# Six tiles for the first evictions, V's weights asked for behind x, two more blocks of Q ahead of the maxima

## The chip, the core and the metric

One core of a Trainium2 chip. Its engines run side by side: TensorE (PE, with its weight loads as PEld), VectorE (DVE), ScalarE (ACT), GpSimd (POOL) and SyncE (SP), which issues nearly all DMAs here. The metric is the device time of one execution in microseconds (us). The kernel before takes 1442.8 us (median of three runs, 1441.62 to 1445.62).

## The reference

Two branches of one input `x` (2048 x 512) are mixed by a gate per token:

```python
x = A_x
g = _sigmoid((x * gate_w).sum(-1, keepdims=True))
a = _A_ref(x, A_wqkv, A_wo)      # attention, 32 heads of 16, full softmax, then @ wo
b = _B_ref(x, B_w_r, ...)        # r = x @ w_r; the two tokens with the largest r
                                 # get a SwiGLU FFN times sigmoid(r); the rest pass x
return g * a + (1 - g) * b
```

Everything is float32. The kernel keeps float32's precision by splitting operands into a high and a low part and adding three products.

## The kernel before

A **unit** is one pair of heads and one half of the 1024-query range: 32 units of 16 **steps** (one step for each block of 128 keys). For every unit the kernel first needs the maxima of the scores (`m_piece`: TensorE products reduced by VectorE), then, some 21 steps behind (`LEAD`), come the scores again (`s_piece`: TensorE, then the exponential on ACT into a tile `P`) and the product with V (`av_mm`). The order of these is written out by hand in `ORDER`, a string that the main loop repeats every three steps: `s` a score piece, `m` a maximum, `A` the product with V, `f` one slot of other work (`slots`: the later projections, the FFN, the output projection). `at_step` hangs small pieces of work on the end of a step; steps of the lead are negative, from -21 to -1. `late` holds ACT work to be issued at the start of the next round of `ORDER`.

The **lead** is what the change touches:

- `load_w(0)` and `load_x` ask for the first weights of K and Q, for x in 16 DMAs, then for constants (`cst`) and V's weights (`wvs`). All these go through SP's queue in order. A DMA of this kernel may wait in SP for the one eight places before it.
- `split_w`, `split_x` make high and low parts: ACT the high, VectorE or POOL the low.
- `proj0` and `proj` multiply out one 512-column block of K or Q for the first four pairs (12 matmuls each into a PSUM tile `st`, of which there are three). The result is split into an eviction tile `ev` (ACT L70, VectorE L71). `first_rows` then copies the first pair's rows by four DMAs into `Kx` or `Qx` (L198, L199), and `store_ev` writes the whole block to a scratch tensor in DRAM (L172). Blocks with an odd number are evicted into `Qx[1]` or `Qx[2]`, which are not in use yet; even ones into the ring tag `ev` with two buffers.
- K's four blocks and Q's first are done up front. `lead_parts` yields the rest in parts of three matmuls: Q's block 1 (four parts), V's first two tiles (a V tile is four parts `v_part`, and ACT evicts it, L270), Q's blocks 2 and 3, the other 14 V tiles.
- The loop over the steps of the lead calls `m_lead` (four products for maxima, L583, and three reductions on VectorE, L588) and three or four of those parts.
- For the gate and the router, `load_rows` loads x by rows in four DMAs (ring tag `xs`, two buffers that x's first two blocks had), `products` multiplies on POOL (L300), `sums` adds up on ACT (L304). `r_row` transposes the router's column on TensorE (L316), and `route_rows`, `route_best`, `route_index` and `gather` find the two tokens.

Ring tags that matter: `xs` (two buffers), `P` (three: x's blocks 2 and 3, V's weights, their low part, later the score tiles), `ev` (two), `st` (three PSUM tiles), `o` (six).

Of the kernel before, what the change touches and what calls it, by code (L numbers as in the profile page):

```python
# [11 lines left out]
OP = mybir.AluOpType  # L12
# [21 lines left out]
def gated_mix(ctx: ExitStack, tc: tile.TileContext, xT, x, wqkv, wo, w_rg, w_gate, w_up, w_down,  # L34
# [9 lines left out]
    def ap(t, off, dims):  # L44
        return bass.AP(tensor=t.tensor, offset=t.offset + off, ap=dims)
# [62 lines left out]
    def load_w(g):  # L108
        ws = ring.tile([128, 2, 4, 128], F32, tag="w", name="ws", bufs=3)
        W[g] = ws  # L110
        for i in (1, 0):
            if g == 0 and i == 0:
                load_x(0)
            nc.sync.dma_start(ws[:, i], ap(wqkv, i * D + g * 128, [[3 * D, 128], [128 * 3 * D, 4], [1, 128]]))

    def split_w(g, parts=(1, 0)):
        if 1 in parts:
# [24 lines left out]
    def proj(g, which, nb, piece):  # L142
        i = "qk".index(which)
        wh, wl = W[g]
        ps = fl_tile() if g else st_tile()
        n = 0
        for terms in (((wh, xh), (wl, xh)), ((wh, xl),)):
            for c in range(4):
                for a, b in terms:
                    nc.tensor.matmul(ps, a[:, i, c, :], b[nb][:, c, :], start=n == 0, stop=n == 11)  # L150
                    n += 1
                    if n % piece == 0 and n < 12:
                        yield
        if g:
            if (g, which, nb) == (2, "q", 3):
                late.append((split_w, (3, (1,))))
                at_step(now[0] + 2, split_w, 3, (0,))
            late.append((evict, (g, which, nb, ps)))
            yield
            return  # L160
        if nb % 2:
            ev = Qx[1 if nb == 3 else 2].rearrange("p (a n) -> p a n", a=2)
        else:
            ev = ring.tile([128, 2, 512], F32R, tag="ev", name="ev", bufs=2)
        scale = 0.25 if which == "q" else 1.0
        split(ev[:, 0], ev[:, 1], ps, scale=scale)
        first_rows(which, nb, ev)
        store_ev(0, which, nb, ev)
        yield

    def store_ev(g, which, nb, ev):
        nc.sync.dma_start(  # L172
            ap(qk_scr[which], g * 128 * S + nb * 512, [[S, 128], [D * S, 2], [1, 512]]).bitcast(F32), ev.bitcast(F32))
# [27 lines left out]
    def proj0(which, nb):  # L201
        for _ in proj(0, which, nb, 12):
            pass
# [6 lines left out]
    load_w(0)  # L210
    for nb in range(1, 4):
        load_x(nb)
    nc.sync.dma_start(cst, consts)
    wvs = ring.tile([128, 4, 512], F32, tag="P", name="wvs", bufs=3)
    nc.sync.dma_start(wvs, ap(wqkv, 2 * D, [[3 * D, 128], [128 * 3 * D, 4], [1, D]]))
    def ones(k):
        for j in range(2):
            nc.gpsimd.memset(k[64 * j + 32:64 * j + 64, :].bitcast(F32), 1.0)
# [9 lines left out]
    split_x(2)  # L228
    proj0("q", 0)
    split_x(3)  # L230
    for nb in (1, 2, 3):
        proj0("k", nb)
    wv = [wvs, Kx[1].rearrange("p (c n) -> p c n", c=4),
          ring.tile([128, 4, 512], F32R, tag="P", name="wvl", bufs=3)]
    for c in range(4):
        split(wv[1][:, c], wv[2][:, c], wvs[:, c], lo_engine=nc.gpsimd if c % 2 else None)

    def load_k(pair):

# [32 lines left out]
    def lead_parts():  # L272

        v = [(t, c) for t in range(KT) for c in range(4)]
        yield from proj(0, "q", 1, 3)
        for n in range(8):
            v_part(*v.pop(0))
            yield
        for nb in (2, 3):
            yield from proj(0, "q", nb, 3)  # L280
        while v:
            v_part(*v.pop(0))
            yield
# [4 lines left out]
    def load_rows(nb):  # L288
        if nb == 0:
            rg["w"] = o_tile("wr", [128, D]), o_tile("wg", [128, D])  # L290
            for i in range(2):
                nc.sync.dma_start(rg["w"][i], ap(w_rg, i * D, [[0, 128], [1, D]]))
        t = ring.tile([128, 4, D], F32, tag="xs", name="xn", bufs=2)
        nc.sync.dma_start(t, ap(x, nb * 512 * D, [[D, 128], [128 * D, 4], [1, D]]))
        rg[nb] = t

# [17 lines left out]
    def r_row():  # L314
        ps = fl_tile((16, 128))
        nc.tensor.transpose(ps, gz[:, :, 0], ident)  # L316
        rg["row"] = ring.tile([16, 128], F32, tag="rt", name="rt", bufs=1)
        nc.scalar.activation(rg["row"], ps, AF.Copy)

    def route_rows():  # L320

# [6 lines left out]
        nc.sync.dma_start(ap(i_scr, 0, [[8, 16], [1, 8]]), idx8)  # L328

    def route_best():  # L330
        nc.vector.max(best8, cand)
        nc.vector.max_index(pos8, best8, cand)
        nc.sync.dma_start(pos2, pos8[:, 0:2])
        nc.sync.dma_start(rsel, best8[:, 0:2])
# [5 lines left out]
    def gather():  # L340
        nc.gpsimd.indirect_dma_start(out=xsel, out_offset=None, in_=x,
                                     in_offset=bass.IndirectOffsetOnAxis(ap=idx2[:, :1], axis=0))
        nc.gpsimd.memset(xselT, 0.0)
        nc.scalar.activation(rsel, rsel, AF.Exp, scale=-1.0)
        nc.vector.tensor_scalar(rsel, rsel, 1.0, None, op0=OP.add)
        nc.vector.reciprocal(rsel, rsel)

    def x_rows():
        ps = fl_tile((128, 4, 2))
# [247 lines left out]
    def m_unit(u):  # L597
        m = ring.tile([128, 2, 8], F32, tag="m", name="m", bufs=2)
        nc.vector.tensor_reduce(m, Mr[:, EL * (u % 3):EL * (u % 3) + EL].rearrange("p (t c j) -> p j t c", c=4, j=2),  # L599
                                axis=AX.X, op=OP.min)  # L600
        hl = ring.tile([128, 2, 2, 8], F32R, tag="hl", name="hl", bufs=2)
        pool_split(hl[:, :, 0], hl[:, :, 1], m)
        turn.append([3 if u < UNITS - 1 else 0, u, hl])

    turn = []
# [155 lines left out]
        for f, a in fill.pop(s, []):  # L761
            f(*a)

    for nb in range(4):
        at_step(-20 + 4 * nb, load_rows, nb)
    for t in range(16):
        at_step(-17 + t, sums, t)
    for t in range(16):
        at_step(-19 + t, products, t)
    at_step(-1, r_row)  # L770
    at_step(1, gates, 0)
    at_step(2, route_rows)
    at_step(4, gates, 1)
    at_step(10, route_best)
    at_step(16, route_index)
    at_step(22, gather)
    at_step(-8, load_w, 1)
    at_step(-5, split_w, 1)
    at_step(2, load_w, 2)
# [9 lines left out]
    order = [(w, nb) for nb in range(4) for w in "kq"]  # L789

    def slots():
        for w, nb in order:
            yield from proj(1, w, nb, 3)
        late.append((split_w, (2,)))
        at_step(now[0] + 4, load_w, 3)
        x_rows()
        yield
        for w, nb in order:
            yield from proj(2, w, nb, 3)
        for n, (w, nb) in enumerate(order):  # L800
            yield from proj(3, w, nb, 3)
            if w == "q":
                for i in range(4):
                    at_step(now[0] + i + 1, load_ff, ("gate", "up")[i // 2], (w_gate, w_up)[i // 2],
                            ("xh", "xl")[i // 2], nb, i % 2)
        yield from ff_in("gate")
        for j in range(4):
            at_step(now[0] + 2 * j, load_down, j)
        ff_t(0, "gate")
        yield  # L810
        yield from ff_in("up")
        ff_t(1, "up")
        late.append((ff_act, ()))
        at_step(now[0] + 3, ff_h)
        at_step(now[0] + 3, load_wo)
        for c in range(4):
            at_step(now[0] + 6 + c, split_wo, c)
        yield
        yield
        yield from ff_down()  # L820
        ff_sum()
        last_tiles()
        s = now[0]
        for nb in range(4):
            at_step(s + 5 + 2 * nb, load_acc, nb)
        for t in range(16):
            at_step(s + 11 + t, acc_scale, t)
        at_step(s + 1, load_at, 0, (0, 1))
        at_step(s + 4, split_at, 0, (0, 1))
        yield from wait(s + 8)  # L830
        yield from wo_groups((0, 1), (2,))
        assert now[0] > 3 * 8 * KT + 16
        yield from wo_groups((2,))
        yield from wait(STEPS - 15)
        for t in range(8, 16):
            wo_last(t, 96)
            yield
# [51 lines left out]
        for _ in range(n):  # L889
            next(parts, None)  # L890

    parts_next(4)
    for s in range(-LEAD, 0):
        now[0] = s
        if s == -11:
            load_q(1)
        m_lead(s + LEAD)
        parts_next(3 + (s < -LEAD + 4))
        end_step(s)
    count["m"] = 4 * LEAD  # L900

    while count["m"] < UNITS * EL:
        run_late()
        for o in ORDER:
            if o == "s":
                s, i = divmod(count["s"], 4)
                if i == 0:
                    start_step(s)
                s_piece(s, i % 2, i // 2)
                count["s"] += 1  # L910
                if i == 3:
                    end_step(s)
            elif o == "m":
                m_next()
            elif o == "A":
                if count["A"] < 0:
                    parts_next(3)
                p_v(count["A"])
                count["A"] += 1
            else:  # L920
                next(fills, None)
# [43 lines left out]
```

## Time and profile before

| | us |
|---|---|
| median of three runs | 1442.8 |
| the profiled execution, as timed | 1443.71 |
| its span, first to last instruction | 1441.9 |
| TensorE busy in the span | 1426.5 |
| VectorE, ACT, POOL busy | 1300.1, 1168.7, 302.5 |
| granted TensorE clock, mean | 0.998 |

The profile shows one execution. Its views used here: the page (busy time of each engine), windows (busy time by stretch, granted clock, DMA rate), the chain of waits that ended last, and timelines of an engine, where a bracket gives the idle time before an instruction and what ended it. Line numbers are those of the kernel before.

### The profile page before, as it was taken

The numbers are of one execution on the slowest core, as the hardware profiler recorded it, in microseconds if no ns is written. First come the engines' busy times: TensorE is split into PE (matmuls) and PEld (weight loads), VectorE is DVE, ScalarE is ACT, GpSimd is POOL, SyncE is SP. The second block draws the span as 40 slices with busy tenths as digits, with TensorE's granted clock in tenths as the row PEclk, the third lists the DMA queues.
The fourth block names the chain that finished last, engine by engine and source line by source line (L and its number), as shares of the span: only waits on it lengthen the run. The fifth ranks groups of instructions, "written<-read, shape, count | busy, mean of one in ns | idle before, by whom it ended". The sixth has DMA issues, their size and how long they took to land.

```text
span 1441.9 us, 24169 instructions
## 1 busy us (share of the span) xinstructions
PE 1426.5 (99%) x9141; PEld 631.9 (44%) x9141; DVE 1300.1 (90%) x1541; ACT 1168.7 (81%) x2262; POOL 302.5 (21%) x321
## 2 busy tenths in 40 slices
PE   8999999999999999999999999999999999999998
PEld 5654444444444444444444443434444444444434
DVE  5779999999999999999999999999999999999933
ACT  4468888888888888888888888888888888888874
POOL 3652000112000001200001100033832222233220
PEclk9999999999999999999999999999999999999999
DMA  8702021212214121312222342314213121111003
GB/s 265 195 21 64 20 52 31 53 45 41 53 53 107 61 53 31 67 31 64 57 81 52 98 104 70 86 42 130 73 31 68 35 53 27 32 31 38 25 17 117
DMA packets 53475, 92.71 MB, mean 64 GB/s; under 512 B 12972, under 2 KB 24300, under 8 KB 51856
## 3 DMA queue, kind: packets, MB, share of 16 engines
q1 hardware_dynamic: 53264, 91.17, 24.4%
q8 instruction: 72, 1.18, 0.4%
q14 instruction: 43, 0.35, 0.1%
q0 software_dynamic: 96, 0.01, 0.0%
HBM read 63.64 MB, written 28.56 MB: 64 GB/s over the span
## 4 chain that ended last, share of the span: by engine, by line
PE 95%; DMA 2%; DVE 1%; SPq 1%; ACT 0%; issue 0%; POOL 0%; DVEq 0%; POOLq 0%; ACTq 0%
PE av L633 35%; PE st L624 23%; PE mxa L556 12%; PE mxb L556 10%; PE fl L150 6%; PE fl L481 4%; PE st L268 3%; DMA xs<-xT 1%; PE mxa L583 1%; DVE Mr L560 1%; DMA wvs<-wqkv 1%; PE fl L372 0%; DVE acc L529 0%; PE st L150 0%; ACT P L625 0%; SPq L615 0%
## 5 line engine op out<-in xcount | busy, mean ns | idle before, releaser
L625 ACT ACTIVATE P<-st 128x512 f32<-128x512 f32 x2028 | 1064.5, 599 | 206.9 <-PE st L624 112.9
L560 DVE TENSOR_REDUCE Mr<-mxa 128x2 f32<-128x1024 f32 x655 | 794.9, 1214 | 3.8 <-PE mxa L556 3.5
L633 PE MATMUL av<-P,V 128*32 128x512 f32 x4096 | 545.5, 605 | 0.0
L624 PE MATMUL st<-Qx,Kx 50*128 50x512 f32 x2028 | 536.2, 443 | 2.0 <-ACT P L625 2.0
L560 DVE TENSOR_REDUCE Mr<-mxb 128x1 f32<-128x512 f32 x654 | 451.9, 691 | 63.5 <-PE st L624 18.1
L624 PEld LDWEIGHTS st<-Qx,Kx 50*128 50x128 f32 x2028 | 274.6, 184 | 234.6 <-ACT P L625 215.0
L556 PE MATMUL mxb<-Kx,Qx 48*128 48x512 f32 x654 | 325.3, 497 | 0.0
L556 PE MATMUL mxa<-Kx,Qx 48*128 48x512 f32 x1310 | 296.7, 420 | 1.2 <-DVE Mr L560 1.2
L556 PEld LDWEIGHTS mxb<-Kx,Qx 48*128 48x128 f32 x654 | 119.5, 183 | 273.7 <-DVE Mr L560 254.4
L556 PEld LDWEIGHTS mxa<-Kx,Qx 48*128 48x128 f32 x1310 | 125.1, 183 | 52.2 <-DVE Mr L560 10.3
L633 PEld LDWEIGHTS av<-P,V 128*32 128x32 f32 x4096 | 80.9, 108 | 140.3 <-issue 134.7
L186 POOL TENSOR_SCALAR ev<-pe 128x512 fp32r<-128x512 f32 x24 | 35.7, 1490 | 321.3 <-ACT pe L184 321.3
L74 POOL TENSOR_SCALAR hl<-m 128x16 fp32r<-128x16 f32 x32 | 8.1, 253 | 441.1 <-DVE m L599 441.0
L448 POOL TENSOR_TENSOR acc<-acc,w 128x512 f32<-128x512 f32 x32 | 41.0, 1281 | 185.8 <-ACT w L447 171.6
L150 PE MATMUL fl<-xh,wh 128*128 128x512 f32 x96 | 42.9, 447 | 0.0
L150 PE MATMUL fl<-xh,wl 128*128 128x512 f32 x96 | 40.4, 421 | 0.0
L529 DVE SCALAR_TENSOR_TENSOR acc<-fl,gg,acc 128x512 f32<-128x512 f32 x15 | 11.3, 750 | 26.6 <-PE fl L481 26.6
L481 PE MATMUL fl<-woh,ahl 128*128 128x512 f32 x96 | 35.1, 447 | 0.0
L588 DVE TENSOR_REDUCE Mr<-mxa 128x2 f32<-128x1024 f32 x21 | 25.7, 1223 | 9.8 <-PE mxa L583 9.8
L150 PE MATMUL fl<-xl,wh 128*128 128x512 f32 x96 | 32.6, 421 | 0.0
L187 POOL TENSOR_TENSOR ev<-pe,ev 128x512 fp32r<-128x512 f32 x24 | 30.8, 1283 | 2.0
L270 ACT ACTIVATE V<-st 128x512 f32<-128x512 f32 x16 | 9.6, 598 | 25.4 <-PE st L268 25.4
(177 smaller groups left out, 781.4 us busy)
## 6 DMA issues: line engine op xcount, KB each, us to landing
Qx<-q_scr SPq DMA_DIRECT2D x62, 128.0 KB
Kx<-k_scr SPq DMA_DIRECT2D x30, 256.0 KB
k_scr<-ev SPq DMA_DIRECT2D x14, 512.0 KB
q_scr<-ev SPq DMA_DIRECT2D x14, 512.0 KB
xs<-xT SPq DMA_DIRECT2D x16, 256.0 KB
xn<-x SPq DMA_DIRECT2D x4, 1024.0 KB
Qx<-hr SPq DMA_DIRECT2D x256, 2.0 KB
acc<-x_scr SPq DMA_DIRECT2D x4, 1024.0 KB
```

Source lines behind the costliest of these rows:

```text
L150: nc.tensor.matmul(ps, a[:, i, c, :], b[nb][:, c, :], start=n == 0, stop=n == 11)
L186: nc.gpsimd.tensor_scalar(ev[:, 0], t, 1.0, None, op0=OP.mult)
L187: nc.gpsimd.tensor_sub(ev[:, 1], t, ev[:, 0].bitcast(F32))
L268: nc.tensor.matmul(ps, a[nb][:, c, sl], b[:, c, :], start=c == 0 and n == 0, stop=c == 3 and n == 2)
L448: nc.gpsimd.tensor_add(a, a, w)
L481: nc.tensor.matmul(ps, a[:, sl], b[:a.shape[0], c, :], start=first and n == 0, stop=last and n == 2)
L556: nc.tensor.matmul(dst, Qx[u % 3][64 * j:64 * j + 48, t * 128:t * 128 + 128], Kx[(u // 2) % 2][64 * j:64 * j + 48, c * 512:c * 512 + 512], ...
L560: nc.vector.tensor_reduce(Mr[:, g0:g0 + (2 if r == 1 else 1)], MX[r - 1], axis=AX.X, op=OP.max, negate=True)
L588: nc.vector.tensor_reduce(*r, axis=AX.X, op=OP.max, negate=True)
L624: nc.tensor.matmul(ps, k, q, start=True, stop=True)
L625: nc.scalar.activation(P[s][:, 2 * j + c, :], ps, AF.Exp)
L633: nc.tensor.matmul(AV[0][32 * ct:32 * ct + 32, :], V[:, kt, h * VW:h * VW + 32], P[s][:, ct, :], start=kt == 0, stop=kt == KT - 1)
```

## The change

Eviction: the blocks of K and Q of the first group get up to six tiles: two from `ev`, and two tiles of tag `xs` that hold two evictions each (`ev0`). The stores to scratch of K's blocks are collected in `scr` and issued behind the row copies of the next Q block. Order: after Q's first block only K's block 1 comes ahead of the split of V's weights; then K's blocks 2 and 3 and Q's 1 and 2 run ahead of the first maxima; only Q's block 3 stays in the lead. V's weights are asked for directly behind x; the constants move to just ahead of the lead's loop. All four low parts of V's weights are made on POOL. x's first two row blocks are loaded into tag `P`, ahead of Q's block 2 being stored; `products` and `sums` are hung one step earlier. The router's transpose is the first of the fill slots, and its other work moves accordingly. Unit 0's split of the maxima is on VectorE. On the host, the weights of K, Q and V are laid out in the order in which they are loaded (2 KB, and 8 KB for V, in one piece for each partition, where there were pieces of 512 bytes and of 2 KB).

```diff
-            nc.sync.dma_start(ws[:, i], ap(wqkv, i * D + g * 128, [[3 * D, 128], [128 * 3 * D, 4], [1, 128]]))
+            nc.sync.dma_start(ws[:, i], ap(wqkv, (2 * g + i) * 128 * D, [[D, 128], [128, 4], [1, 128]]))
...
-        if nb % 2:
-            ev = Qx[1 if nb == 3 else 2].rearrange("p (a n) -> p a n", a=2)
-        else:
-            ev = ring.tile([128, 2, 512], F32R, tag="ev", name="ev", bufs=2)
+        ev = ev0(which, nb)
         scale = 0.25 if which == "q" else 1.0
         split(ev[:, 0], ev[:, 1], ps, scale=scale)
         first_rows(which, nb, ev)
-        store_ev(0, which, nb, ev)
+        scr.append((0, which, nb, ev))
+        if which == "q":
+            if nb == 2:
+                load_rows(0)
+                load_rows(1)
+            for e in scr:
+                store_ev(*e)
+            scr.clear()
         yield
+    scr, evs = [], []
+    def ev0(which, nb):
+        if (which, nb) in (("k", 1), ("k", 3)):
+            t = ring.tile([128, 2, 2, 512], F32R, tag="xs", name="evx", bufs=2)
+            evs.extend([t[:, 0], t[:, 1]])
+        if evs:
+            return evs.pop(0)
+        return ring.tile([128, 2, 512], F32R, tag="ev", name="ev", bufs=2)
...
-    nc.sync.dma_start(cst, consts)
     wvs = ring.tile([128, 4, 512], F32, tag="P", name="wvs", bufs=3)
-    nc.sync.dma_start(wvs, ap(wqkv, 2 * D, [[3 * D, 128], [128 * 3 * D, 4], [1, D]]))
+    nc.sync.dma_start(wvs, ap(wqkv, 8 * 128 * D, [[4 * D, 128], [D, 4], [1, D]]))
...
-    for nb in (1, 2, 3):
-        proj0("k", nb)
+    proj0("k", 1)
...
-        split(wv[1][:, c], wv[2][:, c], wvs[:, c], lo_engine=nc.gpsimd if c % 2 else None)
+        split(wv[1][:, c], wv[2][:, c], wvs[:, c], lo_engine=nc.gpsimd)
...
-        yield from proj(0, "q", 1, 3)
-        for n in range(8):
-            v_part(*v.pop(0))
-            yield
-        for nb in (2, 3):
-            yield from proj(0, "q", nb, 3)
+        yield from proj(0, "q", 3, 3)
...
-        t = ring.tile([128, 4, D], F32, tag="xs", name="xn", bufs=2)
+        t = ring.tile([128, 4, D], F32, tag="P" if nb < 2 else "xs", name="xn", bufs=3 if nb < 2 else 2)
...
-        nc.scalar.activation(rg["row"], ps, AF.Copy)
+        late.append((nc.scalar.activation, (rg["row"], ps, AF.Copy)))
...
-    for nb in range(4):
-        at_step(-20 + 4 * nb, load_rows, nb)
+    at_step(-13, load_rows, 2)
+    at_step(-9, load_rows, 3)
     for t in range(16):
-        at_step(-17 + t, sums, t)
+        at_step(-18 + t, sums, t)
     for t in range(16):
-        at_step(-19 + t, products, t)
-    at_step(-1, r_row)
+        at_step(-20 + t, products, t)
...
     def slots():
+        r_row()
+        at_step(now[0] + 2, route_rows)
+        yield
...
-    parts_next(4)
+    for w, nb in (("k", 2), ("k", 3), ("q", 1), ("q", 2)):
+        proj0(w, nb)
+    nc.sync.dma_start(cst, consts)
...
-        parts_next(3 + (s < -LEAD + 4))
+        parts_next(3 + (s == -LEAD))
...
-                    parts_next(3)
+                    parts_next(2)
```

Left out: `route_best` loses its `max`, which is hung three steps earlier; the sigmoid of the two tokens' scores becomes `route_gate`, its addition on POOL and its reciprocal on VectorE five steps later; `pool_split` of unit 0 becomes a copy and a subtraction on VectorE; the host's permutation of `A_wqkv`.

More of the change, by code (lines that the diff above doesn't have):

```diff
@@ L330, in route_best @@
     def route_best():
-        nc.vector.max(best8, cand)
         nc.vector.max_index(pos8, best8, cand)
@@ L343, in gather, with route_gate @@
         nc.gpsimd.memset(xselT, 0.0)
-        nc.scalar.activation(rsel, rsel, AF.Exp, scale=-1.0)
-        nc.vector.tensor_scalar(rsel, rsel, 1.0, None, op0=OP.add)
-        nc.vector.reciprocal(rsel, rsel)
+    def route_gate(i):
+        if i == 0:
+            nc.scalar.activation(rsel, rsel, AF.Exp, scale=-1.0)
+            nc.gpsimd.tensor_scalar(rsel, rsel, 1.0, None, op0=OP.add)
+        else:
+            nc.vector.reciprocal(rsel, rsel)
     def x_rows():
@@ L601, in m_unit @@
         hl = ring.tile([128, 2, 2, 8], F32R, tag="hl", name="hl", bufs=2)
-        pool_split(hl[:, :, 0], hl[:, :, 1], m)
+        if u == 0:
+            nc.vector.tensor_copy(hl[:, :, 0], m)
+            nc.vector.tensor_sub(hl[:, :, 1], m, hl[:, :, 0].bitcast(F32))
+        else:
+            pool_split(hl[:, :, 0], hl[:, :, 1], m)
         turn.append([3 if u < UNITS - 1 else 0, u, hl])
@@ L762, in end_step @@
             f(*a)
-    for nb in range(4):
-        at_step(-20 + 4 * nb, load_rows, nb)
+    at_step(-13, load_rows, 2)
+    at_step(-9, load_rows, 3)
     for t in range(16):
-        at_step(-17 + t, sums, t)
+        at_step(-18 + t, sums, t)
     for t in range(16):
-        at_step(-19 + t, products, t)
-    at_step(-1, r_row)
+        at_step(-20 + t, products, t)
     at_step(1, gates, 0)
-    at_step(2, route_rows)
     at_step(4, gates, 1)
-    at_step(10, route_best)
-    at_step(16, route_index)
-    at_step(22, gather)
+    at_step(9, nc.vector.max, best8, cand)
+    at_step(12, route_best)
+    at_step(22, route_gate, 0)
+    at_step(27, route_gate, 1)
+    at_step(18, route_index)
+    at_step(24, gather)
     at_step(-8, load_w, 1)
@@ L949 @@
     consts[:, 134] = 128 * p
+    w = np.asarray(inputs["A_wqkv"]).reshape(4, 128, 3, 4, 128)
+    wqkv = np.concatenate([w[:, :, :2].transpose(3, 2, 1, 0, 4).ravel(), w[:, :, 2].transpose(1, 0, 2, 3).ravel()])
     arrays = {
-        "xT": np.ascontiguousarray(x.T), "x": x, "wqkv": np.ascontiguousarray(inputs["A_wqkv"]),
+        "xT": np.ascontiguousarray(x.T), "x": x, "wqkv": wqkv,
         "wo": np.ascontiguousarray(inputs["A_wo"]),
```

## The prediction

> **What bounds the kernel now.** I read the page first, then the windows by stage, then the chain of waits in order of time, and last TensorE's own timeline where the chain leaves it.
>
> ```profile
> span 1441.9 us, 24169 instructions
> PE 1426.5 (99%) x9141; PEld 631.9 (44%) x9141; DVE 1300.1 (90%) x1541; ACT 1168.7 (81%) x2262; POOL 302.5 (21%) x321
> core 0: us, PE busy (x) PEld busy (x) DVE busy (x) ACT busy (x) POOL busy (x), PEclk, DMA share, GB/s
> 6.25:24.17 17.92, 17.55 (x74) 13.13 (x72) 11.85 (x18) 12.23 (x22) 5.82 (x4) 1.00 0.98 338
> 24.17:33.30 9.13, 5.46 (x22) 3.25 (x21) 5.60 (x8) 2.88 (x6) 3.09 (x2) 0.99 0.80 190
> 33.30:95.00 61.70, 61.70 (x269) 40.97 (x268) 49.78 (x65) 29.97 (x81) 43.11 (x36) 0.97 0.51 137
> 140.00:1400.00 1260.00, 1257.71 (x8309) 536.80 (x8305) 1177.69 (x1376) 1064.90 (x2043) 232.84 (x255) 1.00 0.22 55
> 1400.00:1442.00 42.00, 35.78 (x205) 16.56 (x197) 16.15 (x27) 21.80 (x44) 2.57 (x2) 0.97 0.27 100
> ```
>
> TensorE is the bound, with 2.3 us idle in the 1260 us of the main loop, so nothing in the lead matters unless it takes idle or slow time from TensorE. The one stage with idle time that the change touches is 24.17 to 33.30 (3.7 us of 9.1). The tail's 6.2 us idle is not touched.
>
> ```profile
> 13.07 7.56 DMA wvs<-wqkv
> 20.65 0.59 SPq L198
> ...
> 27.85 1.78 DMA Kx<-ev
> 29.67 0.60 ACT Qx L70
> 30.30 0.69 DVE Qx L71
> 30.99 1.14 DVE Mr L588
> 32.18 0.51 PE mxa L583 x2
> 33.32 4.45 PE st L268 x12
> ...
> 41.37 0.43 PE mxa L583 x2
> ...
> 44.98 0.43 PE mxa L583 x2
> ...
> 47.92 0.43 PE mxa L583 x2
> 48.62 2.27 PE st L268 x9
> 50.89 0.43 PE mxa L583 x2
> ```
>
> SP waits for V's weights until 20.65 and then issues eleven copies, one each 0.655 us (20.65 to 27.85). The eviction of Q's second block (L70) waits for the copies out of the buffer it reuses, VectorE's half of it (L71) stands ahead of the first maxima (L588), and TensorE waits for those. TensorE's timeline gives the two gaps, the window after them the clock:
>
> ```profile
> 26.36 0.46 PE L583 MATMUL fl<-Kx,Qx 48*128 48x512 f32 x1 [1.68 <-DMA Kx<-Qx]
> 32.18 0.51 PE L583 MATMUL mxa<-Kx,Qx 48*128 48x512 f32 x2 [1.98 <-DVE Mr L588]
> 33.28:36.70 3.42, 3.42 (x10) 2.70 (x10) 2.37 (x4) 0.00 (x0) 0.00 (x0) 0.53 0.86 215
> 94.73 0.27 PE L316 MATMUL fl<-cst,gz 128*16 128x128 f32 x1
> 96.11 0.50 PE L624 MATMUL st<-Qx,Kx 50*128 50x512 f32 x1 [0.68 <-ACT P L625]
> ```
>
> **What the first stage would take unobstructed.** A step of the lead with three V parts takes 2.97 (47.92 to 50.89), of which 2.27 are nine matmuls, or 0.757 a part; the later steps take 2.93, so its maxima cost 0.66. A step with a whole Q block takes 3.61 (41.37 to 44.98): 2.95 beside the maxima. From 24.17 to 94.73 the old lead does 21 steps of maxima (13.9), two Q blocks (5.9) and 59 V parts (44.7): 64.4 us of work in 70.6. So 6.2 us are lost: 3.7 in the two gaps, some 1.4 to the halved clock (twelve matmuls in 4.45 where 3.03 is the pace), the rest in slow maxima beside the gaps.
>
> **Part 1: evictions, order, queue.** Six buffers take away the wait of L70, and the old VectorE chain with it. SP's order becomes: rows of K0 and Q0, their two stores, sixteen row copies (K1, K2, K3, Q1), four stores, the two rows of the router, then x's rows 0 and 1. SP still stands at Q0's last row copy until V's weights have landed. I put that landing at 20.0 instead of 20.65:
>
> ```profile
> 2.00:2.50 0.50, 0.50 (x3) 0.23 (x2) 0.00 (x0) 0.00 (x1) 0.50 (x1) 1.00 0.68 194
> 10.00:12.00 2.00, 2.00 (x9) 1.51 (x9) 2.00 (x4) 1.89 (x4) 0.00 (x0) 1.00 1.04 400
> 15.92 0.39 PE L150 MATMUL st<-xh,wh 128*128 128x512 f32 x1
> ...
> 18.64 0.39 PE L150 MATMUL st<-xh,wh 128*128 128x512 f32 x1
> ```
>
> The first window holds only the weights' 512-byte pieces: 285 GB/s when all engines are busy (194/0.68), against 385 for x's 2 KB pieces (400/1.04). For 256 KB that is 0.92 against 0.68 us, so two loads give 0.5; the constants (67.5 KB, now asked for later, first used at the router's transpose after the lead) give 0.17 more. The bounds are 0 and 1.4 (the same at 194 and 400 without the shares). TensorE's first products wait for x, so Q's second block ends about 0.4 earlier, at 23.75. [...]
>
> Then Q's third block (2.72, the spacing of two blocks, 15.92 to 18.64) runs where the first gap was, until 26.47. The first two K1 copies are issued 0.65 earlier than now but behind one more store of 512 KB, 1.33 us at the 393 GB/s below: 0.7 later than now, at 27.05, where TensorE wants them at 26.9. I take 0.15 us. VectorE's halves of K2, K3, Q1 and Q2 are done by 27.8 at the latest (26.47, and 0.60 and 0.69 as L70 and L71 took), and the maxima behind them follow with 0.5 us of slack a step (row at 77.76 below), so nothing waits there. The rest of the lead is 21 steps (13.9), the last Q block (2.95) and 60 V parts (45.4): it would end at 88.7 where the old one ends at 94.73, with one V part more behind it.
>
> **Part 2: the new wait.** The sums of the router and gate (L304, ACT) are asked for one step earlier, and stand in ACT's order ahead of V's evictions: the third V tile (V2) behind sums 0, V3 behind sums 1 and 2. ACT stops there until POOL has multiplied, and POOL until x's first rows are in. Behind ACT wait V2 and V3, and with three PSUM buffers TensorE's V5 needs V2 gone and V6 needs V3 gone.
>
> ```profile
> 35.98 0.58 SPq L172 DMA_DIRECT2D q_scr<-Qx  x1
> 36.61 0.47 SPq L292 DMA_DIRECT2D wr<-w_rg  x1
> 34.00:34.50 0.50, 0.50 (x3) 0.40 (x2) 0.50 (x2) 0.00 (x0) 0.00 (x0) 0.50 1.03 393
> 38.00:40.50 2.50, 2.50 (x13) 1.80 (x10) 2.26 (x3) 0.40 (x1) 0.00 (x0) 1.00 1.17 108
> 24.67:26.36 1.69, 0.01 (x3) 0.03 (x1) 1.54 (x2) 1.22 (x3) 1.38 (x2) 1.00 0.70 125
> 24.98 3.09 POOL L68 TENSOR_TENSOR wvl<-wvs,Kx 128x512 fp32r<-128x512 f32 x2 [5.43 <-ACT Kx L67]
> 46.61 1.29 POOL L300 TENSOR_TENSOR p<-xn,wr 128x512 f32<-128x512 f32 x1 [18.54 <-DMA xn<-x]
> 47.87 1.28 POOL L300 TENSOR_TENSOR p<-xn,wg 128x512 f32<-128x512 f32 x1
> 49.81 0.58 ACT L270 ACTIVATE V<-st 128x512 f32<-128x512 f32 x1
> 77.76 1.23 DVE L588 TENSOR_REDUCE Mr<-mxa 128x2 f32<-128x1024 f32 x1 [0.51 <-PE mxa L583]
> ```
>
> Now, Q1's store is issued at 35.98 and POOL starts 10.6 us later: store, the two router rows (at 108 GB/s, the slow part) and x's rows. In the new order the first of four stores is the nineteenth issue after 20.0, at 32.45, and three stores (4.0 us at 393 GB/s) stand ahead of Q1's. POOL starts at 32.45 + 4.0 + 10.6 = 47.1. V2 is out 3.8 us after POOL's start (46.61 to 50.39), at 50.9; V3 has four more products of 1.25 ahead of it: 8.8 after, at 55.9. TensorE wants V5 at 26.47 + 3.6 + 6 x 2.93 + 0.66 + 1.51 = 49.8 and V6 at 26.47 + 3.6 + 8 x 2.93 + 0.66 = 54.2. So it stops for 1.1 us and then 0.6, 1.7 in all. Later tiles keep ahead: four V parts take 3.9 us, the 1.33 pairs of products between them 3.35. From V6 the lead has 2.27 + 11 x 2.93 = 34.5 left: it ends at POOL's start + 43.3 = 90.4. The 0.15 for K1 is inside that.
>
> **Part 3: small edits.** V's four low parts all on POOL: 1.55 each (two in 3.09 at 24.98), 6.2 us from 20.6, done by 27 where V begins at 30; without that cover the wait would be up to 3 us. Unit 0's split on VectorE: two tiny operations (bound 0 to 0.5) inside the 0.51 slack of that stage. The router's transpose (0.27) leaves the lead's end for a fill slot; every later fill group moves three steps back, which the list's wait before its last groups takes up (bound: one slot, 0.9 us). The router's vector operations moved or split: 0 to 0.35 gained. In the first main steps one V tile half open no longer holds a score buffer: of the 0.68 at 96.11 I count 0.4 back, against the missing V part as a bound (0.76 lost).
>
> **Sum.** Old end of lead 94.73, new 90.4: 4.3. One V part more done by then: 0.75. First main steps: 0.4. Less the transpose in its slot, 0.2. Together 5.25 us. The profiled execution took 1443.7 us, of which 1.8 lie around its span; it comes to 1438.45. Its time is 0.9 above the median of the runs (1442.8), against which I predict 1437.6.
>
> **Rivals.** (B) No stop for the sums: the rows arrive by 45.4, when the router's rows, no longer mixed with stores, run at 385 instead of 108 GB/s (512 KB: 1.4 for 4.9 us). For: the 108 was seen in one place only. Against: both read one 2 KB row for 128 partitions, and that does not change. Then the lead ends at 88.7: 7.0 us, 1435.8. (C) The K1 copies become the wait: the extra store at 125 GB/s (24.67 to 26.36, mixed with row copies) takes 4.2 us, they land at 29.9 instead of 27.05, TensorE stops 3.0 us, and a window at half clock follows as at 33.28 (1.6): the lead ends at 93.3, gain 2.4, 1440.4. [...] Here the clock halved after gaps of 1.7 and 2.0, so I keep it. (D) Slower: the four stores back to back run at 125 GB/s. Each takes 4.2 instead of 1.33, POOL starts 11.5 us later, at 58.6, ACT holds V2 and V3, and TensorE stops about 13 us: 6.2 us lost, 1449.0. It is slower than now from a POOL start of 52.3 on. For: 125 is in the trace. Against: there SP's issues, not the stores, set the rate; at 34.0 a store ran at 393.
>
> **How the numbers follow.** Forecast 0.48 (POOL's start good to 1.2 us: 1436.4 to 1438.8), B 0.25, C 0.20, D 0.07. The range runs from B less the 0.35 of the router, 1435.2, to C with 0.6 for the missing V part, 1441.0; outside are D and the edges of B and C. A measurement of this kernel tells 0.3%, 4.3 us, from no change: faster means below 1438.5. That has 0.7 of the forecast, most of B and a little of C: 0.61. Slower by as much is most of D, 0.05. Within: 0.34.
>
> **What would show it.** No wait of L70 for a copy before 30 us, no gap above 0.5 us on TensorE until 48, no clock under 1.0 after 6; POOL's first product at 47.1 (45 to 48.3); two waits of TensorE for V's evictions, 1.1 near 50 and 0.6 near 55; lead's end near 90.4. A first product before 45.4 makes B, a gap for K1 near 27 makes C; a first product after 52, or a stop at the main loop's unit starts, makes me wrong altogether.

## The result, and the profile after

| | before | after |
|---|---|---|
| median of six runs, us | 1444.2 | 1454.43 |
| lowest to highest | 1441.62 to 1447.26 | 1453.86 to 1455.21 |
| span of the profiled execution | 1441.9 | 1452.1 |
| first exponential of the main loop (ACT) | 95.46 | 103.48 |

The ratio is 1.0074 (interval 1.0063 to 1.0084): the changed kernel is slower by some 10 us, where 5 us of gain were forecast. The line numbers from here on are those of the changed kernel, or of the experiment that is named.

The page and the windows of the kernel after, in the columns of before:

```profile
span 1452.1 us, 24171 instructions
PE 1429.4 (98%) x9141; PEld 632.4 (44%) x9141; DVE 1308.4 (90%) x1540; ACT 1169.7 (81%) x2262; POOL 304.0 (21%) x322
...
24.17:33.30 9.13, 7.39 (x32) 4.93 (x31) 4.08 (x6) 1.22 (x3) 2.09 (x2) 1.00 0.65 120
33.30:95.00 61.70, 52.53 (x226) 34.07 (x223) 51.97 (x57) 29.04 (x75) 42.31 (x34) 0.94 0.50 146
86.50:92.50 6.00, 3.00 (x8) 2.17 (x9) 5.96 (x9) 1.03 (x4) 5.32 (x5) 0.50 0.01 2
89.50:93.00 3.50, 3.50 (x9) 2.57 (x10) 3.50 (x6) 0.00 (x0) 2.40 (x2) 0.50 0.01 1
```

The stage that the change was to clear is better: TensorE is idle for 1.74 us of 24.17 to 33.30 instead of 3.67. The next stage, which had no idle time, now has 9.2 us, and near its end the clock is halved; TensorE works 3.5 us of that time (89.50 to 93.00). The chain of waits says where:

```profile
12.63 7.79 DMA wvs<-wqkv
...
21.61 6.06 DMA q_scr<-ev
...
39.80 9.58 DMA xn<-x
49.51 5.82 POOL p L309 x5
...
57.78 0.49 ACT V L284
...
75.76 2.43 DVE Mr L600 x3
78.47 9.64 DVE hl L615
88.31 1.15 DVE Mr L600
89.50 0.80 PE mxa L595 x2
```

One instruction on 128x16 elements, the copy that makes the high part of unit 0's maxima (L615), takes 9.6 us. VectorE's and POOL's timelines beside each other:

```profile
78.22 0.22 DVE L611 TENSOR_REDUCE m<-Mr 128x16 f32<-128x64 f32 x1
78.47 9.63 DVE L615 CAST hl<-m 128x16 fp32r<-128x16 f32 x1
88.14 0.17 DVE L616 TENSOR_TENSOR hl<-m,hl 128x16 fp32r<-128x16 f32 x1
```
```profile
85.58 1.27 POOL L309 TENSOR_TENSOR p<-xn,wg 128x512 f32<-128x512 f32 x1
86.80 1.27 POOL L309 TENSOR_TENSOR p<-xn,wr 128x512 f32<-128x512 f32 x1
88.15 1.29 POOL L309 TENSOR_TENSOR p<-xn,wg 128x512 f32<-128x512 f32 x1
```

POOL's products follow each other every 1.25 us from 49.51 to 89.44; the only place where one does not start on its predecessor's end is 88.07 to 88.15, and there the copy ends. The maxima of the next step stand behind it on VectorE, and TensorE waits for their buffers. TensorE's waits, in total, times, longest:

```profile
PE mxa L595 <- DVE Mr L600: 8.3, 1, 8.3
...
PE fl L595 <- DMA Kx<-evx: 1.1, 1, 1.1
...
PE st L282 <- ACT V L284: 0.8, 2, 0.4
```

### The profile page after: what moved, and what is told of

Same layout as the page of the kernel before. It is cut to its first block, busy times and chain, and to the rows that moved or that the text cites. A ratio compares the mean times of both kernels' runs of the same rounds, so it can differ in the third digit from the quotient of the medians.

```text
span 1452.1 us, 24171 instructions
## 1 busy us (share of the span) xinstructions
PE 1429.4 (98%) x9141; PEld 632.4 (44%) x9141; DVE 1308.4 (90%) x1540; ACT 1169.7 (81%) x2262; POOL 304.0 (21%) x322
## 4 chain that ended last, share of the span: by engine, by line
PE 92%; DMA 2%; DVE 2%; SPq 1%; POOL 1%; ACT 0%; issue 0%; DVEq 0%; ACTq 0%; POOLq 0%
PE av L649 34%; PE st L640 23%; PE mxa L568 12%; PE mxb L568 10%; PE fl L150 6%; PE fl L493 4%; PE st L282 2%; DVE hl L615 1%; DMA xn<-x 1%; DMA wvs<-wqkv 1%; DMA xs<-xT 0%; PE fl L384 0%; POOL p L309 0%; DMA q_scr<-ev 0%; DVE acc L541 0%
## 5 line engine op out<-in xcount | busy, mean ns | idle before, releaser
L313 ACT ACTIVATE p<-p 128x512 f32<-128x512 f32 x32 | 20.2, 631 | 18.3 <-POOL p L309 17.9
```

## The experiments

**Is it the copy, or the place it reads from?** e1 replaces the copy by a second reduction of the same values.

```diff
-            nc.vector.tensor_copy(hl[:, :, 0], m)
+            nc.vector.tensor_reduce(hl[:, :, 0], Mr[:, 0:EL].rearrange("p (t c j) -> p j t c", c=4, j=2),
+                                    axis=AX.X, op=OP.min)
```

> The changed kernel, with unit 0's high part written by a second reduction from Mr (a TENSOR_REDUCE, 0.22 us) instead of the VectorE copy that took 9.63 us; nothing else moves. Theory T1 (VectorE's copy was held by POOL's gapless products, and the lead stood behind it): the 10.9 us between 81.2 and 103.6 come back, the profile shows no VectorE instruction of that line above 1.5 us, the clock stays at 1.0, 1443.5 us (1442.5 to 1444.5). Rival R1 (the copy only sits where VectorE would have waited anyway, because the row products are late): less than 3 us gained, above 1451.

Measured: 1454.63 us, ratio to before 1.0068 (1.005 to 1.0086). The forecast of 1443.5 was missed, and the trace says why. VectorE's timeline of e1:

```profile
80.36 0.21 DVE L615 TENSOR_REDUCE hl<-Mr 128x16 fp32r<-128x64 f32 x1
80.60 8.50 DVE L617 TENSOR_TENSOR hl<-m,hl 128x16 fp32r<-128x16 f32 x1
```

The reduction is not held (0.21 us), but the subtraction behind it is, 8.50 us, until 89.10; POOL's gap in this run is at 89.06 to 89.14. So it is not a matter of the copy. Both held operations lie wholly in SBUF, the one a copy, the other with two tensors read.

**Is it VectorE's doing?** e2 puts unit 0's split back on POOL; e3 is the kernel before with only this split on VectorE.

```diff
-        if u == 0:
-            nc.vector.tensor_copy(hl[:, :, 0], m)
-            nc.vector.tensor_sub(hl[:, :, 1], m, hl[:, :, 0].bitcast(F32))
-        else:
-            pool_split(hl[:, :, 0], hl[:, :, 1], m)
+        pool_split(hl[:, :, 0], hl[:, :, 1], m)
```

> The changed kernel with unit 0's split back on POOL, as before the change. T1: the split stands in POOL's queue behind 28 products that begin at 49.5, so it is done near 85; VectorE's transpose (L626) waits for it, TensorE stops about 5 us instead of 8.3, and the clock may drop for one window: 1449 us (1447 to 1451). Rival R1: no gain, 1454. Rival R4 (POOL's place is free, as it was before): no stop, 1443.5.

> The kernel before with only unit 0's split moved to VectorE, by the same two instructions. T1: in that kernel POOL's products have gaps of 0.5 to 0.7 us near 77 to 82 because ACT holds them up, so the copy is held until the next gap only, 0.3 to 2 us, most of it in VectorE's slack: the copy lasts under 2.5 us and the time is the same within 1 us. Rival R2 (this copy costs 9 us whatever POOL does): about 10 us slower, 1454.

Measured: e2 1448.31 us, 1.0025 (1.0015 to 1.0036); e3 1444.17, 1.0013 (0.9984 to 1.0041), the same as before. VectorE of e2, then VectorE and POOL of e3:

```profile
86.14 0.21 DVE L622 STREAM_TRANSPOSE hr<-hl 128x32 f32<-128x32 f32 x1 [3.88 <-POOL hl L75]
```
```profile
80.11 0.18 DVE L603 CAST hl<-m 128x16 fp32r<-128x16 f32 x1
80.32 0.18 DVE L604 TENSOR_TENSOR hl<-m,hl 128x16 fp32r<-128x16 f32 x1
```
```profile
78.82 1.28 POOL L300 TENSOR_TENSOR p<-xn,wg 128x512 f32<-128x512 f32 x1
81.19 1.29 POOL L300 TENSOR_TENSOR p<-xn,wr 128x512 f32<-128x512 f32 x1 [1.09 <-ACT p L304]
```

In e2 the split queues behind products on POOL, VectorE waits 3.88 us for it, and the kernel is slower than before still, as forecast (1447 to 1451). In e3 the same two instructions on VectorE take 0.18 us each; POOL stood still from 80.10 to 81.19, waiting for ACT. The split in itself was harmless in the old schedule; what the change adds is a POOL that has no gaps.

**The sharp test.** e5 moves one tile of 128x16 elements: unit 0's minima go to PSUM. The copy then reads no SBUF, the subtraction one operand of it.

```diff
+        if u == 0:
+            m = mxb_tile()[:, :16].rearrange("p (j t) -> p j t", j=2)
+        else:
+            m = ring.tile([128, 2, 8], F32, tag="m", name="m", bufs=2)
-        m = ring.tile([128, 2, 8], F32, tag="m", name="m", bufs=2)
```

> The changed kernel with one tile moved: unit 0's minima m (128x16) are written to a PSUM bank instead of SBUF, so that the copy (high part) reads PSUM only and the subtraction (low part) reads one operand from PSUM and one from SBUF. Both stay on VectorE, at the same step. Theory T1 (the two operations are held because they need a second SBUF read path that a gapless run of POOL products keeps): neither is held, copy and subtraction 0.1 to 0.25 us each, TensorE's stop of 8.34 us before the following scores and the 6.83 us of halved clock are gone; 1454.4 - 8.3 - 3.4 + some 1 that the router's and maxima's own pace gives back = 1443.9 us (1442.5 to 1445.5), so no better than the kernel before, because the shifted fill slots still cost some 3. Rival R1 (any small VectorE operation at that place is held while POOL runs, wherever its operands lie): 8 to 10 us for one of the two, 1454.5. Rival R3 (the copy is held because of what a copy is, the subtraction because of its two SBUF operands): copy 8 to 10 us, 1454.5, subtraction 0.2.

Measured: 1444.7 us, 1.0004 (0.9991 to 1.0016), 9.7 less than the changed kernel. VectorE and POOL of e5:

```profile
79.43 0.17 DVE L618 CAST hl<-mxb 128x16 fp32r<-128x16 f32 x1
79.64 0.17 DVE L619 TENSOR_TENSOR hl<-mxb,hl 128x16 fp32r<-128x16 f32 x1
```
```profile
77.85 1.29 POOL L309 TENSOR_TENSOR p<-xn,wr 128x512 f32<-128x512 f32 x1
79.11 1.26 POOL L309 TENSOR_TENSOR p<-xn,wg 128x512 f32<-128x512 f32 x1
80.34 1.29 POOL L309 TENSOR_TENSOR p<-xn,wr 128x512 f32<-128x512 f32 x1
```

Same engine, same step, POOL as busy as in the changed kernel, and nothing is held; the time lies in the forecast range. The cause is shown: the SBUF reads of the two instructions beside POOL's products. A second read path that POOL keeps, by which T1 explained them, was the author's guess; no run shows one.

POOL's small gap is here too, further on, with no held instruction beside it:

```profile
87.82 1.30 POOL L309 TENSOR_TENSOR p<-xn,wr 128x512 f32<-128x512 f32 x1
89.19 1.30 POOL L309 TENSOR_TENSOR p<-xn,wg 128x512 f32<-128x512 f32 x1
```

It stands ahead of POOL's last product in the changed kernel, in e1, e4 and e9 (both below) too, and in the kernel before (90.31 to 90.39). So it is not made by the copy or subtraction that gets through. In the four kernels with a hold of 6 us or more the held instruction ended inside this gap (at 88.10, 89.10, 89.09 and 82.63).

**How long is the hold?** e9 is the changed kernel with the router's first loads ahead of the four stores, which starts POOL's run earlier. e10 leaves out the products with the router's and gate's weights and has POOL copy the rows instead, so that each POOL operation reads one tensor.

```diff
-            if nb == 2:
-                load_rows(0)
-                load_rows(1)
+            if nb in (1, 2):
+                load_rows(nb - 1)
```
```diff
-            nc.gpsimd.tensor_mul(rg["p", t][i], rg[t // 4][:, t % 4, :], rg["w"][i])
+            nc.gpsimd.tensor_scalar(rg["p", t][i], rg[t // 4][:, t % 4, :], 1.0, None, op0=OP.mult)
```

> The changed kernel with one edit: the router's first loads issued ahead of the four stores, as in e7_rows_first; unit 0's split stays on VectorE in SBUF and the fill slots stay shifted. In e7 POOL's products start 5.7 us earlier (43.8 us) and, having caught up with what they wait for, leave gaps at 79.2 and 81.9 us. Theory T1 in its sharp form (the held operation waits for the first gap in POOL's work, not for a time of its own): the copy starts at about 79 and is held for at most 3.5 us instead of 9.63; TensorE stops by 0 to 2.5 us there with at most one window of halved clock; 1446.5 us (1444 to 1449.5). Rival R5 (the hold has a length of its own, or lasts for a number of POOL's instructions): 8 to 10 us again, 1453.6. Rival R6 (the hold lasts one POOL instruction and the rest of it is something else): at most 1.3 us, 1444.

> The changed kernel with POOL's 32 products replaced by a copy of x's rows through a multiplication by 1.0, an operation of POOL with one tensor read instead of two; the products with the router's and gate's weights are left out, so the output is not the reference's. By the rows of the kernel such an operation takes 1.49 us instead of 1.28, so POOL's run of 32 ends some 7 us later, at about 97 us. Theory T1a (any SBUF work of POOL without gaps holds the second read path): the copy on VectorE is held until POOL's first gap, near 95 us, 14 to 17 us, TensorE stops by 13 to 16, and the time is 1460 us or more. Theory T1b (only POOL operations with two tensor reads hold it): the copy takes 0.2 us, no stop there; the sums lag by up to 0.2 us each, so that V evictions wait some more; 1445 to 1449.

Measured: e9 1448.19 us, 1.002 (1.0004 to 1.0036); e10 1449.45, 1.0049 (1.0026 to 1.0071). VectorE and POOL of e9, then VectorE and POOL of e10:

```profile
76.56 6.07 DVE L614 CAST hl<-m 128x16 fp32r<-128x16 f32 x1
```
```profile
81.31 1.28 POOL L308 TENSOR_TENSOR p<-xn,wr 128x512 f32<-128x512 f32 x1
82.68 1.29 POOL L308 TENSOR_TENSOR p<-xn,wg 128x512 f32<-128x512 f32 x1
```
```profile
80.50 0.66 DVE L615 CAST hl<-m 128x16 fp32r<-128x16 f32 x1
```
```profile
74.70 11.68 POOL L309 TENSOR_SCALAR p<-xn 128x512 f32<-128x512 f32 x8
```

In e9 the gaps that e7 (below) had at 79 and 82 us did not come, so the size was missed (6.07 where at most 3.5 was written); but POOL's first gap from there on, 82.59 to 82.68, is where the copy ends, 5.5 us earlier than in the changed kernel. A hold of fixed length, of one POOL instruction or of a fixed number of them is out: with the one under way it lasted through five products in e9 and eight in the changed kernel. As the gap stands ahead of POOL's last product both times, it is not shown that a gap elsewhere would end the hold as well.

In e10 POOL has no gap at all between 49.95 and 96.56, but the copy is held for 0.66 us only, less than one of POOL's 1.46 (11.68 over 8), and it ends in the middle of one (80.52 to 82.01). Neither theory had that number (14 to 17, or 0.2). The long hold goes with POOL's two-tensor products and not with this one-tensor operation. This is one run, and the kind of operation changed together with the number of tensors, so it is not shown which of the two decides. e10's time is no price of that, since its POOL run is longer, TensorE waits elsewhere, and the mean clock of its profiled execution was 0.994 (0.997 in the changed kernel).

**The fill slots.** e4 is e1 with the router's transpose back at the end of the lead, its row's copy behind it and the fill slots unshifted; e6 does the same to e5.

```diff
     def slots():
-        r_row()
-        at_step(now[0] + 2, route_rows)
-        yield
...
-        late.append((nc.scalar.activation, (rg["row"], ps, AF.Copy)))
+        nc.scalar.activation(rg["row"], ps, AF.Copy)
...
+    at_step(-1, r_row)
...
+    at_step(2, route_rows)
```

> e1 with the router's transpose back at the end of the lead, so that all fill slots stand where they stood before the change. Theory T2 (one slot's shift makes ACT's eviction of a fill block meet the eviction of a unit's output once in three units, 0.48 us each, 8 times, 3.7 us in the main loop): 3.7 us faster than e1, about 1439.8, and the main loop's distance to the kernel before stays constant from unit 4 on. Rival R3 (these 3.7 us come from something else in the main loop): within 1 us of e1.

> e5_m_in_psum with the router's transposition back at step -1 of the lead, the row's copy right behind it and the fill slots unshifted, as in the kernel before. T1 and T2 (the shift of the fill slots by one costs some 2.5 to 3 us spread over the main steps, 0.5 at every third unit): 1443.9 - 2.7 = 1441.2 us (1440.0 to 1442.6), and the distance to the kernel before stays flat over the main steps. Rival: the slot's cost came only with the late lead; then as e5, 1443.9.

Measured: e4 1452.1 us, 1.0059 (1.0036 to 1.0082), 2.5 less than e1 where 3.7 was forecast; the 1439.8 written for it was missed, as the subtraction is held in e4 too (9.50 us). e6 1441.13, 0.9986 (0.997 to 1.0001), 3.6 less than e5. Set against the kernel before, exponential by exponential, e5 loses 3.3 us from the 256th to the 1792nd, and e6 gains 0.2. Where such a loss arises is seen on ACT at the end of a unit, first in the kernel after, then in the kernel before:

```profile
400.94 0.60 ACT L662 ACTIVATE o<-av 128x512 f32<-128x512 f32 x1
401.44 0.59 ACT L199 ACTIVATE pe<-fl 128x512 f32<-128x512 f32 x1
401.91 3.06 ACT L641 ACTIVATE P<-st 128x512 f32<-128x512 f32 x6
```
```profile
395.36 0.60 ACT L646 ACTIVATE o<-av 128x512 f32<-128x512 f32 x1
395.86 1.57 ACT L625 ACTIVATE P<-st 128x512 f32<-128x512 f32 x3
```

After, the eviction of a fill block (L199) falls right behind the unit's own output (L662), and ACT then works through six exponentials without a pause: it is behind, and the next score matmuls come late. Before, the fill block is evicted elsewhere. One slot's shift makes these two meet at every third unit's end from 400.9 to 1272.8 us, eight times, where in the kernel before they meet twice. At the six others the distance to the kernel before grows by 0.45 to 0.6 us each, and hardly between them.

**The rest of the lead.** e7 is e6 with the loads of e9. e8 is e7 with the stores of K0 and Q0 behind K1's row copies.

```diff
-        if which == "q":
-            if nb in (1, 2):
+        if which == "q" and nb or (which, nb) == ("k", 1):
+            if which == "q" and nb < 3:
                 load_rows(nb - 1)
-            for e in scr:
+            n = 2 if which == "k" else len(scr)
+            for e in scr[:n]:
                 store_ev(*e)
-            scr.clear()
+            del scr[:n]
```

> e6_psum_no_shift with the router's first loads (both weight rows and x's first 512 rows) issued ahead of the four stores of the split parts (K1, K2, K3, Q1) instead of behind them. Theory T3 (POOL's first product, at 49.5 us, is late because these loads queue behind 2 MB of stores, and the sums that wait for it stop two V evictions by 0.43 and 0.39): first product at 42 to 45.5 us, both stops gone, lead end 0.8 us earlier, 1440.4 us (1439.4 to 1441.8). Rival: POOL is not what sets the lead's end, the lower parts of V on it end at 41.5 anyway and the later stores collide with what follows; 1441.2 or more, the stops 0.4 each or shifted to another place.

> e7_rows_first with the stores of K0 and Q0 (1 MB, which the trace shows issued at 21.0 and 21.6 us) behind the row copies of K1 instead of ahead of them. Theory T4 (K1's copies are late by 1.12 and 0.62 us because 1 MB of stores goes through the DMA engines ahead of them): the two TensorE gaps at 27 to 30 us shrink from 1.74 to at most 0.4, and the lead ends 1.2 to 1.7 us earlier; 1439.0 us (1437.8 to 1440.4). Rival: the copies are limited by their issue on SyncE, 0.6 us each, and not by the stores; the gaps stay at 1.5 to 1.8 and the time at 1440.4.

Measured: e7 1441.58 us, 0.997 (0.9954 to 0.9986); e8 1437.98, 0.9957 (0.9941 to 0.9972). POOL's first product in e7, and TensorE where it waits for K1:

```profile
43.80 1.29 POOL L308 TENSOR_TENSOR p<-xn,wr 128x512 f32<-128x512 f32 x1 [17.41 <-DMA xn<-x]
```
```profile
28.61 0.46 PE L594 MATMUL fl<-Kx,Qx 48*128 48x512 f32 x1 [0.59 <-DMA Kx<-evx]
29.68 0.50 PE L594 MATMUL av<-Kx,Qx 48*128 48x512 f32 x1 [0.60 <-DMA Kx<-evx]
```
```profile
30.30:33.70 3.40, 3.40 (x9) 2.66 (x9) 0.98 (x2) 0.00 (x0) 0.00 (x0) 0.50 0.45 77
```

In e7 POOL starts 5.7 us earlier than in the changed kernel and TensorE's stops for V's evictions (0.92 and 0.46 us in e6) are gone, as written, yet the time is that of e6. Its profiled execution was the longest of ten (1445.51): behind the two gaps for K1 the clock was halved for 3.4 us, some 1.7 us of work, and again for 10.2 us from 1385.4 on, some 5.1. What the other nine did has no profile, so why the median did not move stays open. In e8 the gaps for K1 are gone too, as forecast (1437.8 to 1440.4):

```profile
24.17:33.30 9.13, 9.13 (x42) 6.32 (x42) 5.76 (x8) 1.60 (x3) 1.46 (x2) 1.00 0.77 167
33.30:95.00 61.70, 60.85 (x267) 38.94 (x268) 49.62 (x66) 34.70 (x88) 42.58 (x34) 1.00 0.49 153
...
90.48 1.52 ACT L644 ACTIVATE P<-st 128x512 f32<-128x512 f32 x3
```

The first exponential comes at 90.48 instead of 95.46. e8 takes 0.43% less than the kernel before, and 16 us less than the changed one.

## Why the prediction was wrong

**The step that failed** is in Part 3: "Unit 0's split on VectorE: two tiny operations (bound 0 to 0.5) inside the 0.51 slack of that stage." It was priced by the size of its tiles, and the cover that it lost was not named: on POOL's queue it had been in order with the products, on VectorE it runs beside them. It took 9.63 us, so that TensorE stood still for 8.34 and then worked at half the clock from 89.50 to 93.00, which loses some 1.75: 10.1 in all. (The half clock lasted 6.83 us, but it began at 86.2, while TensorE stood; e5's forecast, with its 3.4, counted all of it.) e5 took away 9.7; its profiled execution lost some 1.7 to a half clock of its own near 31 us (PEclk 0.87 over 24.17 to 33.30), after a wait of 1.9 for K1. The prediction itself had the other half of the cause, a POOL that multiplies back to back (1.25 a product), but used it only for the sums. The runs show which operations were held: the copy (9.63) and the subtraction (8.50) were, the reduction (0.21) and both with PSUM operands (0.17 each) were not. And they show for how long: one product took 1.29 us, the hold five to eight of them.

**The gaps of before.** Half right: no wait of L70, and the gap of 1.98 behind VectorE is gone. The other, TensorE's wait for K1's copies, is not: 1.68 before, 1.12 and 0.62 now. That no half clock followed is partly luck: with the same kind of wait the profiles of e5 and e7 have one near 30 us (PEclk 0.87 and 0.84 over 24.17 to 33.30, 1.00 in the kernel after).

**K1's copies.** Mis-sized: 0.15 forecast, 1.12 and 0.62 measured. V's weights landed at 20.42, not 20.0, and the two stores ahead were done at 27.67 (21.61 and 6.06 in the chain), 1 MB in 6.7 us or some 157 GB/s, not 393; that the stores make the wait is shown by e8. Rival C had nearly this price (125 GB/s), but a stop of 3.0 where 1.74 came.

**The layout.** Of the 0.65 for V's weights 0.5 came from it. The rates were read rightly. The same stretch of the start, with 512-byte pieces before and 2 KB pieces after:

```profile
2.30:2.70 0.40, 0.40 (x2) 0.15 (x1) 0.00 (x0) 0.00 (x0) 0.35 (x2) 1.00 1.07 276
2.30:2.70 0.40, 0.40 (x2) 0.15 (x1) 0.00 (x0) 0.00 (x0) 0.35 (x2) 1.00 0.96 369
```

That is 258 GB/s (276/1.07) against 384 (369/0.96). But the gain is not seen where it was to count: in the ten profiles with the new layout SP goes on behind V's weights at 19.56 to 21.33 (median 20.6), in the two with the old one at 20.65 and 20.52. No run changed the layout alone, so what took the gain back stays open.

**POOL's start and the sums.** The place was right, two stops at V's evictions; POOL started at 49.51 instead of 47.1. Q1's store was issued at 35.90 (36.45 in the sum), but POOL came 13.6 us behind it instead of 10.6. In 1.8 of these 3.0 SP got to x's rows later, as its issues behind the stores took 1.24 us each (0.47 and 0.84 for the router's rows before):

```profile
37.19 1.24 SPq L301 DMA_DIRECT2D wr<-w_rg  x1
38.47 1.23 SPq L301 DMA_DIRECT2D wg<-w_rg  x1
```

The rest is the landing of x's rows, 9.7 us from issue to POOL's start instead of 8.5. The stops were 0.43 and 0.39 instead of 1.1 and 0.6, as TensorE itself came later. Rival B (rows by 45.4) and rival D (stores at 125 GB/s, POOL at 58.6) did not happen.

**The lead as a whole.** Without the hold it would have ended 10.1 earlier: a first exponential at 93.4 against 95.46, 2.1 gained where 4.3 was written. e5 bears this out: 94.90, less the 1.7 of its half clock. The structure of the sum stood, its size did not: V3 was to be out 8.8 us behind POOL's start, and TensorE goes on at 58.32, 8.8 behind 49.51. POOL's start, 2.4 late, makes the lead end about as much later.

**The fill slots.** Bounded at 0.9 us, cost 3.6 (e5 against e6) or 2.5 (e1 against e4). The bound took the shift for one delay; it is a phase, and the meeting on ACT comes back every third unit.

**First main steps.** Forecast 0.4 and 0.75 for the missing V part; the distance to the kernel before shrinks by 2.4 us over the first 128 exponentials, and by 2.4 to 2.6 over the first 256 in e5 to e9, with the fill slots shifted or not. The lead's open V tile may have cost more than its 0.68 wait; that is not shown, and how the 2.4 divide was not tried.

So in the two profiled executions, 10.2 us apart, the hold loses 10.1 and the slots 3.4 up to the 1792nd exponential, against 2.1 gained in the lead and 2.4 in the first steps; the other 1.2 lie behind the 1792nd exponential and were not followed up. None of the rivals had the cause.

## What to carry to other kernels

Before a small operation is moved to VectorE, look at what POOL does at that moment: where POOL multiplied two SBUF tensors without a pause, a VectorE copy from SBUF (9.63 us) or a subtraction with two SBUF inputs (8.50) waited, with 128x16 elements; a reduction (0.21), or either one with an operand in PSUM (0.17), did not. A change that makes an engine gapless takes away the gaps that others lived on. In a periodic schedule price a shift by the phase that it gives everything behind it, not by its own length; and put the copies that the next matmul wants ahead of stores that nobody awaits.

## What the runs showed of the hardware

- The hold lasted through five to eight back-to-back POOL products (9.63, 8.50, 9.50 and 6.07 us against 1.29 for one) and ended at the POOL gap of 0.08 to 0.09 us ahead of the last product each time. With POOL operations that read one tensor it was 0.66 us (one run). Why one kind of POOL operation lets VectorE in and the other does not stays open, and so does what makes the gap.
- The clock was halved for 3.4 us in e7 after gaps of 0.59 and 0.60 us close together, but not in the kernel after, with gaps of 1.12 and 0.62 at the same place (30.30 to 33.70, PEclk 0.50 and 1.00), nor in e6, with one of 1.0 (PEclk 1.00 over the same 3.4 us). What decides was not settled.
